# Two weight conversions and a few weight preparations moved to other steps in a Mamba-2 scan with an ELU feed-forward block

## The chip, the cores and the metric

The kernel runs on one core of a Trainium2 chip. The metric is device time in microseconds (us) of one execution, measured without the profiler; the median of several executions stands for a kernel. One further execution was recorded by the profiler, and all times of single instructions come from that one. Instants are counted from the start of its span.

The core's engines work side by side, each through its own list of instructions in a fixed order: PE (matrix products; PEld is its loading of weights), DVE (vector work), ACT (activation functions), POOL (general work), and SP, which here only starts transfers. They wait for each other through semaphores.

## The reference, cut to what matters

The first block is a chunked state-space scan over four batches of eight heads and 768 tokens; its output is laid out as 3072 tokens of 256 numbers. The second block is a feed-forward layer.

```python
h = x @ w_in                                  # (3072, 256) @ (256, 2048)
g = np.where(h > 0.0, h, np.exp(np.minimum(h, 0.0)) - 1.0)
return g @ w_out                              # (3072, 2048) @ (2048, 256)
```

The weights arrive as 64-bit floating point numbers. The kernel has to turn each into a 32-bit one by integer and floating point work on the two 32-bit words of the number.

## The kernel before, in words

**Tiling.** The 3072 tokens are cut into twelve blocks of 256, numbered n = 0 to 11 in order of work. The scan makes the transposed input `yT` of two neighbouring blocks at a time. The feed-forward layer of a block has eight pieces of w_in (256 columns each) and eight pieces of w_out (256 rows each).

**Conversion of the weights.** `pieces` lists sixteen pieces: 0 to 7 are w_in and 8 to 15 are w_out, so that piece 14 holds the rows that the seventh group of second-layer products (`l2(n, 6)`) reads, and piece 15 those of the eighth (`l2(n, 7)`). One conversion is `w_take` and `w_give`: ACT takes the absolute value (L196), DVE scales the low words (L209), cuts out the signs (L223), clips (L231) and puts the high word together (L238), and POOL adds the two parts (L248). The last step writes the finished piece, and PE waits for it.

**First layer.** Blocks 0 to 3 use plain 32-bit products (`l1`, L667). From the second half of block 2 on, the kernel splits each operand into two words that PE can multiply in a faster format (`l1_words`, L787): three passes per group, `both` times `both`, high word of w times y1, and low word of w times y0. `words_of_w(i)` makes the high word of a w_in piece on ACT (L736) and the sum of its words on DVE (L737). `low_of_w(i)` makes the low word on POOL in two halves (L843). `words_of_y` and `both_of_y` do the same for the input, mainly on DVE (L759, L762, L772).

**Second layer.** Blocks 0 and 1 use plain products (`l2`, L827). From block 2 on, pairs of blocks are multiplied together by a seven-product scheme (`second`, L902). It needs sums and differences of w_out's quarters: `differences` writes a11 - a21 on POOL (L843), and `sum_weights` or its single steps (L714) then change a21 in place and write two more sums. `differences(i, ..)` therefore has to stand before `sum_weights` of the same i.

**The scan beside it.** `scan_ahead`, `turn_part`, `scaled`, `scores`, `sums`, `states`, `across` and `inside` make the scan of later blocks: exponentials on ACT (`decay`, L521) followed by a masking on POOL for every second call (L526), transposes and masks on DVE (L453, L461), a scaling of B on POOL (`scaled`, L408), and small products on PE (L541, L571, L616, L634).

**Order of work.** The tile framework is in manual mode: the order on each engine is the order in which the Python lines are executed, and nothing is reordered. The part that changes is the loop over j = 0 to 7 (first layer of blocks 2 and 3, four pieces each, and all of `l2(0, ..)`), the loop over j = 8 to 15 (first layer in words of blocks 2 and 3 together, called step i = j - 8, with `l2(1, ..)`), and the lines between that loop and the first round of `for n in range(4, NP, 2)`.

Before the change, in the loop over j, the conversion of the next piece is taken ahead of `l1` and given behind it at j = 0, 2, 3, 4, 5, so pieces 11 to 15. `words_of_y(2)` and `words_of_w(4)` follow at j = 4, `low_of_w(4)` and `both_of_y(2)` at j = 5, four differences at j = 6, `words_of_w(5)` at j = 7, and `low_of_w(5)` at step i = 0. Two differences each are at i = 2 and i = 5.

Of the kernel before, what the change touches and what calls it, by code (L numbers as in the profile page):

```python
# [32 lines left out]
def kernel(  # L33
# [27 lines left out]
    nc = tc.nc  # L61
# [21 lines left out]
    def psum(shape, name):  # L83
        return p_a.tile(shape, F32, tag="a", name=name)
# [76 lines left out]
    pieces = []  # L161
# [41 lines left out]
    def w_low(i, eng, cols=slice(None)):  # L203
        if eng is nc.scalar:
            eng.activation(
                pieces[i][0][:, :, cols], w_words(i)[0][:, :, cols], ACT.Identity,
                scale=2.0 ** -51, bias=two)
        else:
            eng.tensor_scalar(  # L209
                out=pieces[i][0], in0=w_words(i)[0], scalar1=2.0 ** -51, scalar2=2.0,  # L210
                op0=ALU.mult, op1=ALU.add)
# [387 lines left out]
    def shift(n, v):  # L599


        return 2 * D * v if n else 0

    def across(*ns):


        y = [[psum([P, len(ns), 2, Q], "ps_y") for _ in range(2)] for _ in range(2)]
        for u in (1, 0):
            for at, n in enumerate(ns):
                for v in range(2):  # L610
                    Sx = starts.pop((n, u, v), None)
                    if Sx is None:
                        continue
                    for q in range(4):
                        rows, col = slice(32 * q, 32 * q + 32), (64 * q + shift(n, v)) % P
                        nc.tensor.matmul(  # L616
                            out=y[q // 2][v][col:col + 64, at, u],
                            lhsT=Sx[rows].rearrange("p k d -> p (k d)"),
                            rhs=st[n]["cts"][rows, u, Q * v:Q * v + Q],
                            start=(u == 1 and at == 0), stop=False,  # L620
                            tile_position=(32 * q, col), skip_group_check=True)
        return y

    def inside(y, *ns, t=None):

        for t in range(2) if t is None else (t,):
            for at, n in enumerate(ns):
                s = st[n]
                for u in range(2):
                    for v in range(2):  # L630
                        toks = slice(Q * v, Q * v + Q)
                        for q in range(4):
                            h, col = 4 * t + q, (D * q + shift(n, v)) % P
                            nc.tensor.matmul(  # L634
                                out=y[t][v][col:col + D, at, u],
                                lhsT=s["x"][toks, u, D * h:D * (h + 1)],
                                rhs=s["M"][h // 2][toks, u, h % 2], start=False, stop=True,
                                tile_position=(Q * v, col), skip_group_check=True)
            n = ns[0]
            if n // 2 not in yT:  # L640
                yT[n // 2] = ffn.tile([P, KC, 2, 2, P], F32, tag="yT", name="yT")
            out = yT[n // 2][:, t, n % 2:n % 2 + len(ns)]
            for v in range(2):
                k = shift(n, v)
                for at in (0, k) if k else (0,):
                    count, src = P - k, (at + k) % P
                    to, src = out[at:at + count, :, :, Q * v:Q * v + Q], y[t][v][src:src + count]
                    if t and n == 1:
                        nc.vector.tensor_copy(to, src)
                    else:  # L650
                        nc.scalar.copy(out=to, in_=src)
        if t:
            for n in ns:
                st.pop(n)
# [76 lines left out]
    def words_of_w(i):  # L731

        w = pieces[i][0]
        k_words[i] = conv.tile(
            [P, 2, KC, CW], F32R, tag="w64", name="w_words", bufs=W_AHEAD)
        nc.scalar.activation(k_words[i][:, 0], w, ACT.Copy, scale=NEAR)  # L736
        nc.vector.scalar_tensor_tensor(  # L737
            out=k_words[i][:, 1], in0=k_words[i][:, 0].bitcast(F32), scalar=1.0 / WORD - 1.0,
            in1=w, op0=ALU.mult, op1=ALU.add)

    def low_of_w(i):

        w0 = conv.tile([P, KC, CW], F32R, tag="w_in", name="w0", bufs=DF // CW + 1)
        for k in range(KC):
            sub(w0[:, k], pieces[i][0][:, k], k_words[i][:, 0, k].bitcast(F32))
        k_words[i] = k_words[i], w0
# [20 lines left out]
    def both_of_y(n):  # L767
        y = yT[n // 2].rearrange("p k b u i -> p k (b u i)")
        y1, y0 = y_words[n]
        both = ffn.tile([P, KC, 2 * BLK], F32R, tag="yT", name="y_both")  # L770
        for k in range(KC):
            nc.vector.scalar_tensor_tensor(  # L772
                out=both[:, k], in0=y1[:, k].bitcast(F32), scalar=1.0 - WORD,
                in1=y[:, k], op0=ALU.mult, op1=ALU.add)
        y_words[n] = y1, y0, both
# [66 lines left out]
    def sub(out, in0, in1):  # L842
        nc.gpsimd.tensor_tensor(out=out, in0=in0, in1=in1, op=ALU.subtract)  # L843
# [120 lines left out]
    def w_take(i, low):  # L964

        w_abs(i)
        w_low(i, low)
        w_sign(i)

    def w_give(i):  # L970

        w_high(i)
        w_sum(i)
# [115 lines left out]
    todo = 5  # L1089
# [77 lines left out]
    def differences(i, count):  # L1167
        for r in range(i, i + count):
            sub(s_out[1][:, r], a_out[0][:, r], a_out[2][:, r])

    for j in range(2 * DIRECT):
        n, i = 2 + j // DIRECT, j % DIRECT
        if j < 7:
            l2(0, j)
        piece = todo < len(pieces) and j != 1
        if j == 0:
            elu()
        if piece:
            w_take(todo, nc.vector)
        l1(n, i)  # L1180
        if j == 7:
            l2(0, j)
        if j == 0:
            scaled(3, nc.gpsimd)
            turn(3)
            elu()
            turn_exp(3)
        if piece:
            w_give(todo)
            todo += 1  # L1190
        while lag:
            elu()
        if j == 0:
            decay(3, 2)
            decay(3, 3)
        if j == 1:
            scores(3)
            sums(3)
            for q in range(4):
                weigh(3, q)  # L1200
        if j == 2:
            states(3)
        if j == 3:
            inside(across(3), 3)
        if j == 4:
            words_of_y(2)
        if j == 4:
            words_of_w(4)
        if j == 5:
            low_of_w(4)  # L1210
        if j == 5:
            both_of_y(2)
        scan_ahead(j)
        if j == 3:
            s_out[:] = weight_sums()
        if j == 6:
            differences(0, 4)
        if j == 7:
            words_of_w(5)
    for j in range(8, 16):  # L1220
        i = j - 8
        l1_words(2, j)
        if i == 7:
            words_of_y(4)
        for p in ((), (6,), (), (7,), (0,), (1,), (2,), ())[i]:
            words_of_w(p)
        for p in ((5,), (), (6,), (7,), (0,), (), (), ())[i]:
            low_of_w(p)
        if i == 7:
            l2(1, 6)  # L1230
            l2(1, 7)
        begin_end()
        if i == 0:
            turn_part(5, 2)
            scaled(4, nc.gpsimd)
            scaled(5, nc.gpsimd)
        if i < 2:
            load_bc(i + 6)
            l2(1, i)
        if i == 2:  # L1240
            turn_part(4, 3)
            turn_part(5, 3)
            scores(4, 5)
            sums(4, 5)
            for q in range(4):
                weigh_two(4, q)
            l2(1, 2)
            states(4)
            states(5)
            for to in (6, 7):  # L1250
                load_b(to)
                spread_cum(to)
        if i == 3:
            l2(1, 3)
        if i == 4:
            l2(1, 4)
            y = across(4, 5)
            inside(y, 4, 5)
        if i == 5:
            l2(1, 5)  # L1260
        if i in (0, 1, 3, 4):
            sum_t1(2, (0, 1, 3, 4).index(i), nc.vector)
        if i in (4, 6):
            turn_part(6, i // 2 - 2)
        if i in (2, 5):
            differences(4 if i == 2 else 6, 2)
        if i < 6:
            sum_weights(nc.gpsimd, a_out, s_out, i)
    both_of_y(4)
    end_words()  # L1270
    words_of_w(3)
    decay(6, 0)
    for p in (3, 1, 2):
        low_of_w(p)
    sum_t2(2, 0)
    sub(g_of[2, 14][:, 1], g_of[2, 14][:, 1], g_of[2, 14][:, 0])
    left = (step for i in (6, 7) for step in weight_steps(nc.vector, a_out, s_out, i))
# [105 lines left out]
```

## Time and profile before

| quantity | value |
|---|---|
| device time, median of 3 runs | 351.92 us (351.70 to 352.15) |
| device time of the profiled execution | 351.6 us |
| its span, first to last instruction | 349.5 us |
| PE busy | 340.5 us (97%) |
| DVE, ACT, POOL busy | 259.7, 234.7, 217.2 us |
| granted clock of PE | 1.000 |

The profiled execution lies 0.3 us below the median, and 2.1 us of it lie outside the span. In the views that follow, a row gives the start, the duration, the engine, the line of the kernel, the operation, what is written from what, the shapes and the number of instructions that are merged in it. A bracket at the end of a row gives idle time ahead of it and the instruction that ended it. A row of waits gives the total, the number of waits and the longest one. Ends of matrix products are modelled, so the text uses the starts of the products: of 128x256 in plain format they start 0.216 us apart, of 128x512 in the faster format 0.232 us apart, when nothing holds them up.

### The profile page before, as it was taken

The numbers are of one execution on the slowest core, as the hardware profiler recorded it, in microseconds if no ns is written. First come the engines' busy times: TensorE is split into PE (matmuls) and PEld (weight loads), VectorE is DVE, ScalarE is ACT, GpSimd is POOL, SyncE is SP. The second block draws the span as 40 slices with busy tenths as digits, with TensorE's granted clock in tenths as the row PEclk, the third lists the DMA queues.
The fourth block names the chain that finished last, engine by engine and source line by source line (L and its number), as shares of the span: only waits on it lengthen the run. The fifth ranks groups of instructions, "written<-read, shape, count | busy, mean of one in ns | idle before, by whom it ended". The sixth has DMA issues, their size and how long they took to land.

```text
span 349.5 us, 9873 instructions
## 1 busy us (share of the span) xinstructions
PE 340.5 (97%) x3878; PEld 298.1 (85%) x3878; DVE 259.7 (74%) x515; ACT 234.7 (67%) x537; POOL 217.2 (62%) x338
## 2 busy tenths in 40 slices
PE   8899999998999999999999999999999999999996
PEld 5579888887778899988989988989988999999996
DVE  3998979879997899876878775888675856665232
ACT  4789989697658888657599457599457466565000
POOL 5554554557999599975196764196854174455760
DMA  8988989381360510070431170330000100001002
GB/s 143 247 213 188 296 171 233 81 148 36 70 138 3 110 46 29 10 158 4 105 62 32 13 155 4 89 50 2 2 0 5 62 0 3 0 0 50 15 0 62
DMA packets 72727, 26.49 MB, mean 76 GB/s; under 512 B 57768, under 2 KB 67560, under 8 KB 72680
## 3 DMA queue, kind: packets, MB, share of 16 engines
q1 hardware_dynamic: 70360, 25.60, 31.8%
q8 instruction: 30, 0.49, 0.6%
q10 hardware_dynamic: 2320, 0.26, 0.5%
q14 instruction: 17, 0.14, 0.1%
HBM read 22.51 MB, written 3.34 MB: 74 GB/s over the span
## 4 chain that ended last, share of the span: by engine, by line
PE 83%; DVE 4%; POOL 3%; ACT 3%; SPq 2%; issue 2%; DMA 2%; POOLq 0%; DVEq 0%; ACTq 0%
PE ps_o L902 36%; PE ps_h L787 18%; PE ps_w L787 9%; PE ps_h L667 9%; PE ps_o L827 4%; PE ps_y L634 2%; PE ps_g L541 2%; DMA w<-in_moe_w_in_dram 2%; PE ps_y L616 1%; PE ps_st L571 1%; POOL L L526 1%; POOL w L843 1%; SPq L178 1%; DVE y L762 1%; POOL w_sum L843 1%
## 5 line engine op out<-in xcount | busy, mean ns | idle before, releaser
L902 PEld LDWEIGHTS ps_o<-w_out,g 128*128 128x128 f32 x640 | 78.5, 191 | 3.4
L902 PE MATMUL ps_o<-w_out,g 128*128 128x128 f32 x640 | 80.1, 275 | 0.0
L800 ACT ACTIVATE e<-ps_h 128x512 f32<-128x512 f32 x72 | 43.0, 598 | 47.0 <-DVE ps_h L794 47.0
L808 DVE SCALAR_TENSOR_TENSOR g<-e,ps_h 128x512 f32<-128x512 f32 x72 | 49.4, 686 | 31.9 <-ACT e L801 31.6
L843 POOL TENSOR_TENSOR g<-g 128x256 f32<-128x256 f32 x36 | 26.5, 737 | 58.3 <-DVE g L808 58.2
L794 DVE SCALAR_TENSOR_TENSOR ps_h<-ps_h,e 128x512 f32<-128x512 f32 x72 | 50.1, 695 | 12.4 <-ACT e L791 9.1
L791 ACT ACTIVATE e<-ps_w 128x512 f32<-128x512 f32 x72 | 42.3, 587 | 19.8 <-PE ps_w L787 19.6
L787 PE MATMUL ps_w<-y_both,w_words 128*128 128x512 f32 x144 | 51.5, 437 | 0.1
L801 ACT ACTIVATE e<-e 128x512 f32<-128x512 f32 x72 | 45.5, 632 | 2.3
L667 PE MATMUL ps_h<-yT,w_in 128*128 128x256 f32 (+1 forms) x208 | 45.1, 367 | 1.6 <-POOL w_in L248 1.6
L787 PE MATMUL ps_h<-y,w_words 128*128 128x512 f32 x144 | 45.7, 399 | 0.0
L787 PE MATMUL ps_h<-y,w 128*128 128x512 f32 x144 | 45.0, 392 | 0.2 <-POOL w L843 0.2
L667 PEld LDWEIGHTS ps_h<-yT,w_in 128*128 128x128 f32 x208 | 36.4, 190 | 7.2 <-POOL w_in L248 2.3
L521 ACT ACTIVATE L<-L,ncum 128x64 f32<-128x64 f32 x160 | 42.2, 336 | 0.2
L902 PE MATMUL ps_o<-w_sum,g 128*128 128x128 f32 x304 | 38.6, 276 | 0.0
L902 PEld LDWEIGHTS ps_o<-w_sum,g 128*128 128x128 f32 x304 | 37.0, 192 | 1.4
L526 POOL TENSOR_SCALAR_AFFINE_SELECT L<-L 64x512 f32<-64x512 f32 x40 | 29.3, 732 | 9.6 <-ACT L L521 8.2
L787 PEld LDWEIGHTS ps_h<-y,w 128*128 128x128 f32 x144 | 27.0, 188 | 7.2 <-POOL w L843 0.7
L787 PEld LDWEIGHTS ps_h<-y,w_words 128*128 128x128 f32 x144 | 26.7, 188 | 6.2 <-issue 0.5
L843 POOL TENSOR_TENSOR g<-t,g 128x256 f32<-128x256 f32 x40 | 28.2, 738 | 5.8 <-PE ps_o L902 5.7
L827 PE MATMUL ps_o<-w_out,g 128*128 128x256 f32 x128 | 30.5, 382 | 1.0 <-POOL w_out L248 1.0
L843 POOL TENSOR_TENSOR g<-g,t 128x256 f32<-128x256 f32 x40 | 28.8, 751 | 0.2
(133 smaller groups left out, 538.9 us busy)
## 6 DMA issues: line engine op xcount, KB each, us to landing
L<-flat SPq DMA_DIRECT2D x20, 256.0 KB
w<-in_moe_w_out_dram SPq DMA_DIRECT2D x8, 512.0 KB
w<-in_moe_w_in_dram SPq DMA_DIRECT2D x7, 512.0 KB
xr<-in_x_dram SPq DMA_DIRECT2D x24, 128.0 KB
out_dram<-c_sum SPq DMA_DIRECT2D x9, 256.0 KB
bc<-in_B_dram SPq DMA_DIRECT2D x24, 64.0 KB
bc<-in_C_dram SPq DMA_DIRECT2D x22, 64.0 KB
ec<-flat_exp SPq DMA_DIRECT2D x10, 128.0 KB
```

What stands on the lines that cost most here:

```text
L521: nc.scalar.activation(L[:, h, u], L[:, h, u], ACT.Exp, bias=ncum[:, u, row:row + 1])
L526: nc.gpsimd.affine_select(out=part, in_=part, pattern=[[0, 4], [0, 2], [1, Q]], compare_op=ALU.is_ge, fill=0.0, base=0, channel_multiplier=-1)
L667: nc.tensor.matmul(out=ps[:, j, toks], lhsT=w_in[i][:, k, j * P:(j + 1) * P], rhs=yT[n // 2][:, k, n % 2].rearrange("p u i -> p (u i)")[:, ...
L787: nc.tensor.matmul(out=ps, lhsT=lhs[:, k], rhs=rhs[:, k], start=k == 0 and lhs is not w0, stop=k == KC - 1 and lhs is not w1)
L791: nc.scalar.activation(e, both, ACT.Copy, scale=WORD)
L794: nc.vector.scalar_tensor_tensor(out=high, in0=high, scalar=WORD - 1.0, in1=e, op0=ALU.mult, op1=ALU.add)
L800: nc.scalar.activation(e, high, ACT.Relu, scale=-1.0)
L801: nc.scalar.activation(e, e, ACT.Exp, scale=-1.0)
L808: nc.vector.scalar_tensor_tensor(out=g_of[n, m].rearrange("p b i -> p (b i)"), in0=e, scalar=1.0, in1=h, op0=ALU.subtract, op1=ALU.max)
L827: nc.tensor.matmul(out=o_of[n][:, ts], lhsT=g_of[n, j][:, m % 2, ts * P:(ts + 1) * P], rhs=w_out[:, m], start=(m == 0 and ts == 0), stop=( ...
L843: nc.gpsimd.tensor_tensor(out=out, in0=in0, in1=in1, op=ALU.subtract)
L902: nc.tensor.matmul(out=ps[:, ts], lhsT=b[:, ts * P:(ts + 1) * P], rhs=a[:, i], start=(i == chunk[0] and ts == 0), stop=(i == chunk[-1]), s ...
```

## The change

Piece 14 is converted as a whole at the end of j = 3, behind `inside(across(3), 3)`, and piece 15 at j = 4 behind `words_of_y(2)`; both were taken at the head of the following j. `words_of_w(4)` moves from j = 4 to j = 5 and stands ahead of `both_of_y(2)`. `words_of_w(5)` and `low_of_w(5)` move to j = 6, from j = 7 and from step i = 0. The differences 0 to 3 move from j = 6 to step i = 0, the differences 4 and 5 stay at i = 2, and 6 and 7 move from i = 5 to behind `low_of_w(3)`, ahead of `low_of_w(1)`. No function changes.

```diff
-        piece = todo < len(pieces) and j != 1
+        piece = j in (0, 2, 3)
...
         if j == 3:
             inside(across(3), 3)
+            w_take(14, nc.vector)
+            w_give(14)
         if j == 4:
             words_of_y(2)
-        if j == 4:
+            w_take(15, nc.vector)
+            w_give(15)
+        if j == 5:
             words_of_w(4)
-        if j == 5:
+            both_of_y(2)
             low_of_w(4)
-        if j == 5:
-            both_of_y(2)
         scan_ahead(j)
...
         if j == 6:
-            differences(0, 4)
-        if j == 7:
             words_of_w(5)
+            low_of_w(5)
...
-        for p in ((5,), (), (6,), (7,), (0,), (), (), ())[i]:
+        for p in ((), (), (6,), (7,), (0,), (), (), ())[i]:
             low_of_w(p)
...
-        if i in (2, 5):
-            differences(4 if i == 2 else 6, 2)
+        if i in (0, 2):
+            differences(4 * (i // 2), 4 - i)
...
-    for p in (3, 1, 2):
-        low_of_w(p)
+    low_of_w(3)
+    differences(6, 2)
+    low_of_w(1)
+    low_of_w(2)
```

## The prediction

> **What bounds the kernel now.** The first view is the busy time of the engines: PE works for 97% of the span, so what can be won is PE's idle time. The second is the list of PE's waits over the whole span, which says whom it waits for; PEld rows are the same stalls seen from the weight load.
>
> ```profile
> PE 340.5 (97%) x3878; PEld 298.1 (85%) x3878; DVE 259.7 (74%) x515; ACT 234.7 (67%) x537; POOL 217.2 (62%) x338
> ```
>
> ```profile
> PE ps_y L634 <- issue: 1.7, 4, 0.6
> PE ps_h L667 <- POOL w_in L248: 1.6, 3, 0.8
> ...
> PE ps_o L827 <- POOL w_out L248: 1.0, 1, 1.0
> PE ps_h L787 <- POOL w L843: 0.2, 1, 0.2
> ```
>
> The w_in row belongs to the start, which the change leaves alone. The one w_out wait is piece 15, and "POOL w L843" is a low word. The third view, the timeline around that wait, shows what delays piece 15: DVE does the words of y and w (75.38, 77.06) and a transpose before its four conversion instructions, and POOL's sum comes at 80.55.
>
> ```profile
> 77.06 1.14 DVE L737 SCALAR_TENSOR_TENSOR w_words<-w_words,w_in 128x512 fp32r<-128x512 f32 x1
> ...
> 78.61 0.41 DVE L209 TENSOR_SCALAR w_out<-w 128x512 f32<-128x512 uint32 x1
> ...
> 79.71 0.69 DVE L238 SCALAR_TENSOR_TENSOR mag<-mag,sgn 128x512 uint32<-128x512 uint32 x1
> ...
> 80.55 1.27 POOL L248 TENSOR_TENSOR w_out<-mag,w_out 128x512 uint32<-128x512 uint32 x1 [2.89 <-DVE mag L238]
> 80.92 2.58 DVE L772 SCALAR_TENSOR_TENSOR y_both<-y,yT 128x512 fp32r<-128x512 f32 x2
> 81.78 2.31 POOL L843 TENSOR_TENSOR w<-w_in,w_words 128x256 fp32r<-128x256 f32 x2
> 81.87 1.59 PEld L827 LDWEIGHTS ps_o<-w_out,g 128*128 128x128 f32 x8 [1.41 <-POOL w_out L248]
> ```
>
> PE's last first-layer product starts at 80.49, so the next could start at 80.70; it starts at 81.87. That stall is **1.17**. Later a product of group (2,10) starts at 91.50 instead of 91.09, waiting for the low word of piece five (POOL's row at 89.97): **0.41**.
>
> The fourth view is POOL's timeline behind the loop: idle until 117.63, then without a pause to 146.
>
> ```profile
> 113.47 0.46 POOL L714 TENSOR_TENSOR w_sum<-w_out,w_sum 128x128 f32<-128x128 f32 x1
> 117.63 5.35 POOL L843 TENSOR_TENSOR w<-w_in,w_words 128x256 fp32r<-128x256 f32 x6 [3.70 <-ACT w_words L736]
> 122.94 2.83 POOL L843 TENSOR_TENSOR t<-g 128x256 f32<-128x256 f32 x4
> ...
> 143.61 1.39 POOL L526 TENSOR_SCALAR_AFFINE_SELECT L<-L 64x512 f32<-64x512 f32 x2
> 145.09 0.64 POOL L408 TENSOR_TENSOR b_tok<-b_tok,eb 128x256 f32<-128x256 f32 x1
> ```
>
> **The change part by part.** No instruction is added or removed, and no DMA is issued at another step: SP's order is untouched, and ACT and POOL start no transfers here. Nothing is priced by its own duration, only by what waits for it.
>
> *Piece 14.* ACT's absolute value (0.67) passes eight exponentials (0.24 apart) and starts at 69.85 instead of 71.78; the next activation, at 72.35, has the same work ahead of it. DVE's clip then runs at 70.6 and its last step ends at 71.7; POOL's sum (1.27) ends at 73.1 instead of 75.06. PE reads the piece at 75.52, so both are hidden. POOL's two maskings (70.99) move behind the sum to 74.5, DVE's transpose (69.18) to 72.3; they are next needed at 95 and 84. Cost 0.
>
> *Piece 15.* ACT's absolute value moves from 75.50 to 74.0, ahead of the word of w. DVE: the words of y start at 74.2 as before. They took 1.11, 0.69 and 1.14; a free one of 128x512 with two operands takes 0.69 (the row of 115.3), so they end between 76.1 and 77.1, the first if POOL is idle, which it is now after 74.5. The four conversion steps take 1.8 (78.61 to 80.40), POOL follows 0.15 later with 1.27: ready between 79.3 and 80.3, needed at 80.70. The cover is 0.4 even at the slow end. **Gain 1.17.**
>
> *Words of w four, both of y, low word of four.* They now follow the conversion, so PE needs them earlier: l2(0,7) would end at 82.43, where the first group in words starts. DVE after 77.9: transpose 0.65, an ELU step 0.68, words of w, two halves of both-of-y. The two halves bound each other with POOL:
>
> ```profile
> L772 DVE SCALAR_TENSOR_TENSOR y_both<-y,yT x2: 687/687/687, 115.3 to 115.9; 128x512 fp32r<-128x512 f32 x2
> ```
> ```profile
> L772 DVE SCALAR_TENSOR_TENSOR y_both<-y,yT x2: 1209/1329/1449, 80.9 to 82.3; 128x512 fp32r<-128x512 f32 x2
> ```
>
> The first row is with POOL idle, the second beside the two low-word instructions: each half ends 0.55 after a POOL instruction ended (81.82, 82.95), and the next POOL instruction ends 0.58 after the half. They take turns. In the new order they meet POOL's sum (to 79.3) and two maskings of 0.67; taking turns gives words of w at 79.84 and the halves at 80.92 and 82.00. Free, they would end at 81.0; with the 1.45 and 1.21 of before, at 82.7. Need 82.43: cost 0 to 0.3, taken 0. The low word follows on POOL, its halves at 82.6 and 83.3, needed at 83.36 and 83.59 (third pass): cost 0 to 0.2, taken 0.
>
> The Trainium skill, "SBUF — State Buffer", section "Who interferes with whom", calls this an exclusive lock of a port that DVE and GpSimd share, held for a whole instruction by whoever starts first, and so says that more POOL work beside DVE costs whole instructions. The rows agree that turns are taken. Read at its worst, with a neighbour of 1.27 instead of 0.67 for both halves, the estimate is 83.2 and a loss of 0.8; by the rows it is 0.
>
> *Words and low word of five.* Their ACT part fills an idle stretch (ACT sat idle for 2.51 ahead of 83.90). DVE's word stands ahead of the last ELU step at 84.3 instead of 87.16; that step waits for its exponential until 84.4 and then 0.5 for the word. POOL's low word (0.79 and 0.73) follows two maskings and ends by 86.9 instead of 91.45; PE needs it at 90.86 - 1.17 = 89.7. **Gain 0.41.** Behind it in POOL's queue wait two maskings and the two scalings of B (0.8 each), done at 89.9 instead of 93.27; the small products that read them stall some 0.1 at 93.24. Gain 0.1.
>
> DVE decides whether this holds: from 87.16 to 100 it has no idle time, and PE's group (2,11) starts at 95.90 and 96.56 right after DVE's second and fourth weighting product (95.76, 96.42). Without the word of five (0.72) and with ACT earlier, DVE's first step there goes from 87.80 to 86.1: 1.7 as well. Between 1.3 and 1.9 by collisions, taken 1.7.
>
> *Differences 0 to 3* leave POOL at 86.03 (2.16) and come after the scalings, at 89.9 to 91.7. The weight sums and the low word of six behind them end at 97.2, needed at 100.22 - 1.7 = 98.5. Cost 0.
>
> *Differences 6 and 7* leave 111.10, where POOL later idles 3.70, and enter the unbroken stretch. Four of them at 86.03 start 0.42 apart; the contended one at 111.52 took 0.92. So POOL is later by 0.83, between 0.8 and 1.85. Next late: the second half of the low word of one, ready at 121.48, goes to 122.27; PE can see it at 122.32 and wants it at 122.19: cost 0.13. Then the scaling of the B of block 7 (row 145.09, ready at 145.73): PE loads it at 145.91, 0.07 after the load before, so the slack is some 0.1. At a lateness of 0.7 (some turns with DVE fall better) PE waits **0.6**; bounds 0, if turns absorb all, and 1.75. DVE's steps 6 and 7 (L714, 125.11) need the differences by then and have them.
>
> Sum: 1.17 + 0.41 + 0.1 - 0.13 - 0.6 = 0.95, so the profiled execution goes from 351.6 to 350.65. The median lies 0.32 above it: **350.95**.
>
> **The rivals.**
> A: the late POOL work is absorbed. For it: about 2 us of that stretch are turns with DVE (118.32 took 1.19 for 0.73), which fall anew. Against: no pause in 28 us. Gain 1.68: 350.25.
> B: DVE comes late at 82 and in the steps that follow, 0.5 in all, by unlucky turns. For it: the small cover of 0.4. Then the gain is 0.45: 351.45, no difference to see.
> C, slower: POOL's stretch from 117.63. Two contended differences (1.85) and two more collisions like the one at 133.74 (1.22 for 0.73, so 0.49 each) make the scaling 2.8 late; PE waits 2.7 at 145.9 and ends 1.1 behind: 353.0. It turns the sign from a lateness of 1.65, and shows as slower from 2.4. Against: only two of the 37 instructions up to the scaling are extra.
> D: the stalls only move, for example into the 0.85 at 104.99, where the profile names "issue" and no engine; gain 0.2: 351.7.
>
> **How the numbers follow.** The forecast has 0.45, A 0.22, B 0.20, C 0.08, D 0.05. Faster by over 0.2% (0.70 us, about what a measurement of this kernel can tell) means below 351.22: A and three quarters and more of the forecast's own range of 350.5 to 351.4, 0.60. Same takes B, D and the rest, 0.31; slower 0.09. The range of 350.0 to 351.8 takes in A, B and D and leaves C out.
>
> **What would show it.** Right: PE's w_out wait is gone; the sum of piece 15 ends before 80.0; the both-of-y rows end by 82.4; PE's wait for "w L843" at 91 is gone; a new PE wait for POOL appears at the sums near 144. Wrong: PE waits for DVE y_both near 82.5, or DVE's weighting products move up by less than 1.3, or the new wait at the sums is absent (A) or above 1.6 (C).

## The result, and the profile after

The changed kernel takes **350.53 us** (median of 7 runs, 349.88 to 351.0) beside 351.92 for the kernel before on the same chip. The ratio is 0.9954 with a 95% interval of 0.9939 to 0.9969: faster by 0.3 to 0.6%. Put beside three other kernels later, it gave 350.41 against 351.74, ratio 0.9966 (0.9952 to 0.998). The forecast was 350.95.

The line of busy times, and the whole list of PE's waits in the changed kernel (us in total, times, longest):

```profile
PE 341.0 (98%) x3878; PEld 298.4 (86%) x3878; DVE 257.9 (74%) x515; ACT 234.7 (67%) x537; POOL 216.5 (62%) x338
```
```profile
PE ps_y L634 <- issue: 1.6, 4, 0.6
PE ps_h L667 <- POOL w_in L248: 1.6, 3, 0.8
PE ps_idle L263 <- DVE idle L258: 1.1, 1, 1.1
```

The wait for w_out (1.0 before) is gone from the list, and so is the one for "w L843" at 91. What stands there still is the start and the "issue" stalls (PE idle while the profile names no engine that it waits for), which the change does not touch. The timeline around the old stall shows why, first in the kernel before, then in the changed one (rows of other work in between are left out):

```profile
73.79 1.27 POOL L248 TENSOR_TENSOR w_out<-mag,w_out 128x512 uint32<-128x512 uint32 x1 [1.40 <-DVE mag L238]
...
74.24 1.11 DVE L759 TENSOR_SCALAR y<-yT 128x512 fp32r<-128x512 f32 x1
...
75.38 1.75 DVE L762 SCALAR_TENSOR_TENSOR y<-y,yT 128x512 fp32r<-128x512 f32 x2
```

```profile
74.57 0.47 DVE L759 TENSOR_SCALAR y<-yT 128x512 fp32r<-128x512 f32 x1
...
75.08 1.29 DVE L762 SCALAR_TENSOR_TENSOR y<-y,yT 128x512 fp32r<-128x512 f32 x2
...
76.29 0.42 DVE L209 TENSOR_SCALAR w_out<-w 128x512 f32<-128x512 uint32 x1
...
78.25 1.28 POOL L248 TENSOR_TENSOR w_out<-mag,w_out 128x512 uint32<-128x512 uint32 x1 [3.49 <-DVE mag L238]
...
79.48 2.19 POOL L526 TENSOR_SCALAR_AFFINE_SELECT L<-L 64x512 f32<-64x512 f32 x2
80.00 2.20 DVE L772 SCALAR_TENSOR_TENSOR y_both<-y,yT 128x512 fp32r<-128x512 f32 x2
...
81.09 1.89 PE L827 MATMUL ps_o<-w_out,g 128*128 128x256 f32 x8
81.75 2.26 POOL L843 TENSOR_TENSOR w<-w_in,w_words 128x256 fp32r<-128x256 f32 x2
...
84.06 0.19 PEld L787 LDWEIGHTS ps_h<-y,w 128*128 128x128 f32 x1 [0.36 <-POOL w L843]
```

Piece 15's sum ends at 79.53; PE reads the piece at 81.09, straight behind its product. The words of y run from 74.57 to 76.37, in 1.80, where they took 2.89 before (74.24 to 77.13), since POOL is idle beside them from 74.76 on. Both of y ends at 82.20, and PE's first group in words starts at 82.63 without a wait for it. The low word of four ends at 84.01, and the third pass of that group waits for its second half at 84.06: a new, small stall.

Three later places carry costs. The first is on DVE (its timeline near 98): the sixth state of blocks 4 and 5 waits 0.71 for POOL's masked states, which stand behind the differences and the low word of six. The first line is POOL's, from its own timeline.

```profile
90.91 1.88 POOL L843 TENSOR_TENSOR w_sum<-w_out 128x128 f32<-128x128 f32 x4
```
```profile
98.36 0.28 DVE L588 SCALAR_TENSOR_TENSOR S_new<-S_new,ec,ps_st 128x64 f32<-128x64 f32 x1 [0.71 <-POOL Sx L593]
98.55 0.68 DVE L808 SCALAR_TENSOR_TENSOR g<-e,ps_h 128x512 f32<-128x512 f32 x1
```

Before, the six states ran through without a wait, and the ELU step behind them began at 99.37:

```profile
97.67 1.79 DVE L588 SCALAR_TENSOR_TENSOR S_new<-S_new,ec,ps_st 128x64 f32<-128x64 f32 x6
...
99.37 0.68 DVE L808 SCALAR_TENSOR_TENSOR g<-e,ps_h 128x512 f32<-128x512 f32 x1
```

So DVE is ahead by 0.82 here, where it was ahead by 1.42 at the first state. The second place follows from it: PE's first group in words of blocks 4 and 5, near 115, waits longer for both of y. The third is POOL's stretch from 116.09, with differences 6 and 7 in it:

```profile
116.09 1.87 POOL L843 TENSOR_TENSOR w<-w_in,w_words 128x256 fp32r<-128x256 f32 x2 [3.41 <-ACT w_words L736]
117.93 1.32 POOL L843 TENSOR_TENSOR w_sum<-w_out 128x128 f32<-128x128 f32 x2
119.21 2.93 POOL L843 TENSOR_TENSOR w<-w_in,w_words 128x256 fp32r<-128x256 f32 x4
...
144.03 0.64 POOL L408 TENSOR_TENSOR b_tok<-b_tok,eb 128x256 f32<-128x256 f32 x1
```

The scaling of block 7's B starts 1.06 sooner than before (145.09), PE's sums there come 1.29 sooner. Within the sums PE's products now stand 0.27 apart ahead of the one at 144.50, where they stood 0.12 apart before. That product still belongs to block 6, and the load for it (144.47) comes 0.12 behind a step of DVE, the last of `c_sum` (to 144.35); in the kernel before, it came 0.12 behind the same step too (to 145.49). In a second profile of the changed kernel (changed_again below) this step is in time, and PE pauses at the change from block 6 to block 7 instead: the two loads stand 0.56 apart, and the second, at 145.16, comes 0.06 behind the end of the scaling.

```profile
143.60 0.75 DVE L880 TENSOR_TENSOR c_sum<-ps_o,c_sum 128x256 f32<-128x256 f32 x2
```
```profile
PE ps_st L571 <- POOL b_tok L408: 0.3, 1, 0.3
```

The first row is from the first profile, the second from the waits of the second. In the first, too, the scaling (to 144.67) would have held block 7's load until some 144.73; it came at 144.77. So two waits of nearly the same size lie on top of each other here.

**How the runs below are compared.** Single parts are worth 0.1 to 0.7 us, and the interval of a ratio is 0.4 to 0.7 us to either side. So the parts are read from PE, whose order is the same in all kernels here: the time between the starts of the same two matmuls, less that time in the kernel before. The stretches, by the clock of the kernel before: a, 80.49 to 82.41, piece 15; b, to 85.30, the first group in words; c, to 92.09, up to the low word of five; d, to 94.33, the sums of blocks 4 and 5; e, to 114.01, without 104.02 to 105.07, which holds an "issue" stall; f, to 117.20, the first group in words of blocks 4 and 5; g, to 143.07; h, to 146.62, the sums of blocks 6 and 7. All in us against the kernel before, with the ratio of the times:

| kernel | a | b | c | d | e | f | g | h | sum | ratio (95%) |
|---|---|---|---|---|---|---|---|---|---|---|
| changed | -1.27 | +.20 | -.52 | -.28 | +.04 | +.24 | +.01 | +.15 | -1.44 | .9954 (.9939, .9969) |
| changed_again | -1.27 | +.27 | -.53 | -.26 | +.08 | +.28 | .00 | +.17 | -1.27 | .9966 (.9952, .9980) |
| conv_alone | -1.27 | +.29 | +.68 | -.29 | -.36 | +.21 | .00 | -.20 | -.94 | .9978 (.9966, .9990) |
| words_alone | -.01 | .00 | -.55 | -.29 | -.03 | +.03 | +.11 | +.24 | -.49 | .9987 (.9972, 1.0002) |
| piece14_back | -1.27 | +.84 | -.51 | -.29 | -.36 | +1.04 | +.01 | -.15 | -.69 | .9969 (.9952, .9987) |
| diff_spread | -1.27 | +.26 | -.53 | -.27 | -.14 | +.25 | .00 | +.19 | -1.50 | .9956 (.9940, .9971) |
| state_bufs | -1.27 | +.27 | -.53 | -.26 | +.09 | +.08 | +.06 | +.27 | -1.29 | .9944 (.9925, .9963) |
| diff67_back | -1.27 | +.26 | -.55 | -.24 | +.10 | +.26 | +.01 | -.20 | -1.64 | .9976 (.9964, .9989) |
| diff67_twice | -1.27 | +.30 | -.53 | -.26 | +.05 | +.30 | +.68 | +.36 | -.37 | .9985 (.9971, 1.0000) |
| low4_early | -1.27 | -.01 | -.55 | +.10 | +.09 | +.27 | +.02 | +.20 | -1.15 | .9959 (.9945, .9973) |
| conv15_first | -1.27 | +.78 | -.55 | -.24 | -.23 | .00 | +.15 | +.32 | -1.05 | .9970 (.9958, .9983) |
| bufs_and_dve | -1.27 | +.27 | -.53 | -.27 | +.06 | .00 | +.71 | +.66 | -.38 | 1.0018 (1.0006, 1.0031) |
| all_three | -1.27 | +.75 | -.52 | -.26 | -.18 | -.01 | +.74 | +.67 | -.09 | 1.0020 (1.0008, 1.0033) |

The first two rows are two profiles of one kernel. They agree within 0.07 in every stretch, and within 0.17 in the sum; a difference below that between two rows is not read. The start, up to 80.49, varies more: it is 0.10 shorter to 0.93 longer than that of the kernel before, in code that no row changes, and the "issue" stall near 104 is 0.38 shorter to 0.14 longer. A profile's own span therefore says less than this sum.

### The profile page after: what moved, and what is told of

Same layout as the page of the kernel before. It is cut to its first block, busy times and chain, and to the rows that moved or that the text cites. A ratio compares the mean times of both kernels' runs of the same rounds, so it can differ in the third digit from the quotient of the medians.

```text
span 348.6 us, 9875 instructions
## 1 busy us (share of the span) xinstructions
PE 341.0 (98%) x3878; PEld 298.4 (86%) x3878; DVE 257.9 (74%) x515; ACT 234.7 (67%) x537; POOL 216.5 (62%) x338
## 4 chain that ended last, share of the span: by engine, by line
PE 87%; ACT 3%; DVE 3%; SPq 2%; DMA 2%; issue 1%; POOL 0%; POOLq 0%; ACTq 0%
PE ps_o L902 36%; PE ps_h L787 18%; PE ps_h L667 11%; PE ps_w L787 9%; PE ps_o L827 6%; PE ps_y L634 2%; DMA w<-in_moe_w_in_dram 2%; PE ps_g L541 2%; PE ps_y L616 1%; PE ps_st L571 1%; DVE ps_h L794 1%; ACT e L800 1%; SPq L178 1%; ACT yT L651 1%; ACT e L801 1%
## 5 line engine op out<-in xcount | busy, mean ns | idle before, releaser
L808 DVE SCALAR_TENSOR_TENSOR g<-e,ps_h 128x512 f32<-128x512 f32 x72 | 49.3, 685 | 31.9 <-ACT e L801 30.4
L843 POOL TENSOR_TENSOR g<-g 128x256 f32<-128x256 f32 x36 | 27.3, 758 | 58.5 <-DVE g L808 58.4
L791 ACT ACTIVATE e<-ps_w 128x512 f32<-128x512 f32 x72 | 42.2, 586 | 20.1 <-PE ps_w L787 20.0
L843 POOL TENSOR_TENSOR g<-t,g 128x256 f32<-128x256 f32 x40 | 28.2, 737 | 5.8 <-PE ps_o L902 5.7
L843 POOL TENSOR_TENSOR g<-g,t 128x256 f32<-128x256 f32 x40 | 28.6, 748 | 0.2
```

Source lines behind the costliest of these rows:

```text
L791: nc.scalar.activation(e, both, ACT.Copy, scale=WORD)
L808: nc.vector.scalar_tensor_tensor(out=g_of[n, m].rearrange("p b i -> p (b i)"), in0=e, scalar=1.0, in1=h, op0=ALU.subtract, op1=ALU.max)
```

## The experiments

The diffs are against the changed kernel.

**The change once more, and its two halves.** The repeat (changed_again) has no edit.

> The changed kernel once more, beside the three others of this group. It tells what of a profile repeats. Expected: from PE's last first-layer product ahead of the second one of piece 15 to the end of the sums of blocks 6 and 7, leaving out the stall within the small products near 104, 1.4 to 1.5 less than the kernel before, as in the first profile; the start and the stalls within the small products differ by up to 0.5. Time 350.5.

Time as expected; the sum came out at 1.27, a little under the 1.4 to 1.5 expected, and the stall left out 0.16 shorter than before.

The conversions alone:

```
         if j == 6:
-            words_of_w(5)
-            low_of_w(5)
+            differences(0, 4)
+        if j == 7:
+            words_of_w(5)
...
-        for p in ((), (), (6,), (7,), (0,), (), (), ())[i]:
+        for p in ((5,), (), (6,), (7,), (0,), (), (), ())[i]:
             low_of_w(p)
...
-        if i in (0, 2):
-            differences(4 * (i // 2), 4 - i)
+        if i in (2, 5):
+            differences(4 if i == 2 else 6, 2)
...
-    differences(6, 2)
```

> Pieces 14 and 15, the words of four and both of y as in the changed kernel; the words and the low word of five and all differences as before. Theory (the conversions bring the 1.17, the words of five the rest): PE's wait for w_out is gone, its wait for the low word of five stays and grows, because PE arrives 1 us sooner and DVE, which still holds the word of five among the last ELU steps, moves by about 1.0 only. Time 350.9 to 351.4, 0.5 to 1.0 below the kernel before and some 0.6 above the changed one. Rival 1 (the conversions bring everything): 350.5, as the changed kernel. Rival 2 (the stall only moves to the low word of five): 351.7 to 351.9.

The words of five and the differences alone:

```
-        piece = j in (0, 2, 3)
+        piece = todo < len(pieces) and j != 1
...
-            w_take(14, nc.vector)
-            w_give(14)
...
-            w_take(15, nc.vector)
-            w_give(15)
-        if j == 5:
             words_of_w(4)
-            both_of_y(2)
+        if j == 5:
             low_of_w(4)
+        if j == 5:
+            both_of_y(2)
```

> The words and low word of five and the differences as in the changed kernel; pieces 14 and 15, the words of four and both of y as before. Theory: PE's wait for w_out stays at 1.0 to 1.2, the 0.41 at the low word of five is gone, the moved differences cost up to 0.4 behind it: 351.5 to 352.0, no difference to the kernel before that can be told. Rival (POOL's and DVE's relief at the words of five brings most of the gain): 351.0 or less.

Measured: 351.04 us for the conversions, 351.27 for the words, beside 351.72. PE's waits from 78 to 95, first with the conversions alone, then with the words alone:

```profile
PE ps_h L787 <- POOL w L843: 0.6, 1, 0.6
```
```profile
PE ps_o L827 <- POOL w_out L248: 1.0, 1, 1.0
```

Each half leaves the other's stall. With the conversions alone the wait for the low word of five grows, as expected of PE coming sooner, but 0.36 of that comes back in e, at the products that started right behind DVE's weighting products before (95.90 and 96.56). The sums are 0.94 and 0.49; together 1.43, beside 1.27 and 1.44 for the whole change. So the two halves add up, two thirds and one third, and both rivals that give all to one half fall. The time of the words alone is 0.2 below the range expected, and the interval of its ratio takes in no change, so for that half the waits and the sum speak, not the time.

**What piece 14's place is worth.**

```
-        piece = j in (0, 2, 3)
+        piece = j in (0, 2, 3, 4)
...
             inside(across(3), 3)
-            w_take(14, nc.vector)
-            w_give(14)
```

> The changed kernel with piece 14 converted around the first-layer product of step 4, as before, and piece 15 at its new place. Theory (only piece 15 was late; piece 14 has over a microsecond in hand wherever it stands): PE has no wait for w_out of over 0.1, time 350.5. Rival (piece 14 had to leave, because its steps stand ahead of the words of y and of piece 15 on DVE and POOL): piece 15's sum ends past PE's need, a wait for w_out of 0.2 to 0.8 comes back, 350.7 to 351.3.

351.14 us beside 352.0. PE has no wait for w_out, as the theory has it, but the first group in words waits 0.84 (b), and the group at f 1.04, where the changed kernel lost 0.2 and 0.24. Neither side expected that. The timeline (DVE and POOL) shows where it starts:

```profile
74.50 1.28 POOL L248 TENSOR_TENSOR w_out<-mag,w_out 128x512 uint32<-128x512 uint32 x1 [1.38 <-DVE mag L238]
74.95 1.11 DVE L759 TENSOR_SCALAR y<-yT 128x512 fp32r<-128x512 f32 x1
76.10 1.29 DVE L762 SCALAR_TENSOR_TENSOR y<-y,yT 128x512 fp32r<-128x512 f32 x2
...
79.22 1.28 POOL L248 TENSOR_TENSOR w_out<-mag,w_out 128x512 uint32<-128x512 uint32 x1 [3.43 <-DVE mag L238]
```

Piece 14's sum now stands on POOL beside DVE's first word of y, as in the kernel before. It has 0.83 left when that word starts, and the word takes 1.11 instead of 0.47 (there POOL's masking had 0.19 left). In the kernel before, in the changed one and here the word ends 0.28 or 0.29 behind POOL's instruction. That 0.64 reaches piece 15 and everything behind it on POOL: its maskings, the low word of four, and the masked states. DVE's wait from 92 to 100:

```profile
DVE S_new L588 <- POOL Sx L593: 1.7, 1, 1.7
```

So moving piece 14 matters, by some 0.6 to 0.75 of the sum, though PE never waited for that piece.

**The differences 0 to 3, and the state that waits.** The first run computes each difference just ahead of the sum that uses it:

```
-        if i in (0, 2):
-            differences(4 * (i // 2), 4 - i)
         if i < 6:
+            differences(i, 1)
             sum_weights(nc.gpsimd, a_out, s_out, i)
```

> The changed kernel, but each of differences 0 to 5 is computed just ahead of the weight sum that needs it, so that one and not four of them stand ahead of the low word of six and the masked states on POOL. Theory: DVE's wait of 0.7 for POOL's Sx at 98.4 is gone or under 0.2, DVE's both-of-y for blocks 4 and 5 ends 0.3 to 0.7 sooner, PE's pause at its first group in words of blocks 4 and 5 falls from 0.24 beyond that of the kernel before to about 0: 350.3, 0.2 below the changed kernel. Rival 1: the state waits for the low word of six itself and not for the differences ahead of it: the 0.7 stays above 0.4, 350.5. Rival 2: the 0.24 is won and is lost again at the sums of blocks 6 and 7 (pause there 0.4): 350.5.

350.3 us beside 351.72. The state's wait falls to 0.3, but f stays at +0.25. Here another thing takes its place, seen on DVE (first fence) and POOL (second):

```profile
112.93 1.55 DVE L762 SCALAR_TENSOR_TENSOR y<-y,yT 128x512 fp32r<-128x512 f32 x2 [0.22 <-ACT y L757]
114.41 1.28 DVE L772 SCALAR_TENSOR_TENSOR y_both<-y,yT 128x512 fp32r<-128x512 f32 x2
```
```profile
113.07 0.87 POOL L714 TENSOR_TENSOR w_sum<-w_out,w_sum 128x128 f32<-128x128 f32 x1
```

POOL's last weight sum meets the low word of y, whose two halves take 1.55 instead of 1.29 (a half 0.94 instead of 0.69). The same is seen with the conversions alone (1.51) and with differences 6 and 7 at step 5 (1.58), and f is +0.21 to +0.26 in all three (in the last the state still waits 0.7). So f was no proof of the state's wait, and the next run asks for it by itself:

```
-            new = att.tile([P, 2, D], F32, tag="S", name="S_new", bufs=6)
+            new = att.tile([P, 2, D], F32, tag="S", name="S_new", bufs=7)
...
-            Sx = att.tile([P, 2, D], F32, tag="Sx", name="Sx", bufs=12)
+            Sx = att.tile([P, 2, D], F32, tag="Sx", name="Sx", bufs=11)
```

> The changed kernel with seven buffers instead of six for the states and eleven instead of twelve for the masked states. It tells what DVE's sixth state of blocks 4 and 5 waits for, and what that wait is worth. Theory A (the sixth state waits for the buffer that POOL's masked states free): the wait of 0.7 is gone, DVE's ELU step behind it starts 0.6 sooner against PE, and the pause of PE at its first group in words of blocks 4 and 5 (0.26 above that of the kernel before) goes to under 0.1. Theory B (POOL's last weight sum sets a floor there, as in the runs with a separate conversion and with spread differences, where one half of the low word of y took 0.91 to 0.94 instead of 0.69): the wait of 0.7 is gone, one half of the low word of y takes over 0.85, and the pause stays at 0.2 to 0.3. Theory C: the wait is no matter of buffers, and stays at 0.6 to 0.7. Time 350.3 by A, 350.5 by B and C.

350.17 us beside 352.0, and DVE's timeline there:

```profile
96.18 1.72 DVE L588 SCALAR_TENSOR_TENSOR S_new<-S_new,ec,ps_st 128x64 f32<-128x64 f32 x6
97.82 0.68 DVE L808 SCALAR_TENSOR_TENSOR g<-e,ps_h 128x512 f32<-128x512 f32 x1
...
112.46 1.39 DVE L762 SCALAR_TENSOR_TENSOR y<-y,yT 128x512 fp32r<-128x512 f32 x2 [0.22 <-ACT y L757]
```

The six states run through without the wait, so it was one for a buffer. f falls to +0.08, and in the two later runs with these buffers to 0.00, while one half of the low word of y loses 0.1 to POOL. That is A, for the most part. But h rises from +0.15 to +0.27, and the sum stays where it was: what PE gains at f it waits for at the sums. The profile gives that wait to DVE's `c_sum`, but the scaling (to 144.62) would have held block 7's load until some 144.68, and it came at 144.70; against the product at f, the scaling comes no sooner than in the changed kernel.

```profile
PE ps_st L571 <- DVE c_sum L880: 0.2, 1, 0.2
```

**The differences 6 and 7.** Back at step 5, and twice in their new place:

```
-        if i in (0, 2):
-            differences(4 * (i // 2), 4 - i)
+        if i in (0, 2, 5):
+            differences(*{0: (0, 4), 2: (4, 2), 5: (6, 2)}[i])
...
-    differences(6, 2)
```

> The changed kernel, but differences 6 and 7 are computed at step 5 again, where POOL idles later. Theory (the trace: the scaling of the B of block 7 is 0.16 late for the sums): the 0.25 pause of PE at the sums of blocks 6 and 7 goes, 350.35, 0.1 to 0.2 below the changed kernel. Rival 1, the forecast's own price (0.6 and 0.13): 349.8. Rival 2, the lateness is only the turns with DVE and comes back elsewhere: 350.5, no change, and the pause stays.

```
     differences(6, 2)
+    differences(6, 2)
```

> The changed kernel with differences 6 and 7 computed twice in their new place, which adds two POOL instructions of 0.45 to 0.92 to the unbroken stretch. Theory (a lateness there counts one for one at the sums of blocks 6 and 7): PE's pause there grows from 0.25 to 1.0 to 1.3, time 351.3. Rival (turns with DVE absorb it): the pause stays under 0.5, time 350.6.

Back at step 5: 350.96 us beside 351.72. The pause at the sums is gone, h is -0.20, 0.35 to 0.37 better than in the two profiles of the changed kernel: both the scaling and `c_sum` are in time. (The 0.16 in the expectation sets the scaling against the product at 144.50, which is block 6's.) The time, 0.6 above the theory's, does not show it, as 0.35 us is less than the interval of the ratio; that the ratio came out above the changed kernel's has no counterpart in these stretches.

Twice: 351.57 us beside 352.0. The waits from 117 to 147:

```profile
PE ps_st L571 <- POOL b_tok L408: 0.5, 1, 0.5
...
PE ps_h L787 <- POOL w L843: 0.2, 1, 0.2
```

Two more instructions (2.16 for the four, 1.32 for the two) cost 0.9 to 1.07 of the sum: one for one, as the theory says, and a little more. But most of it falls at the low word of one (g, +0.68), and only then at the sums (h, +0.36), where the products stand 0.70 apart and not the 1.0 to 1.3 of the theory.

**Attempts to win more.** The low word of four sooner:

```
             w_give(15)
+            words_of_w(4)
+            low_of_w(4)
         if j == 5:
-            words_of_w(4)
             both_of_y(2)
-            low_of_w(4)
```

> The changed kernel with the words and the low word of piece four issued right behind piece 15, ahead of the maskings of that step. Theory: PE's pause of 0.2 at the third pass of its first group in words (wait for the low word of four) is gone, and that is kept to the sums of blocks 4 and 5: 350.3. Rival: the low word now meets the words of w and the halves of both of y on DVE, so the first pass waits for both of y instead, 0.1 to 0.6: 350.5 to 351.0.

350.52 us beside 352.0. The stall at b is gone (-0.01), and both of y is not late. The price comes elsewhere: the sums of blocks 4 and 5 wait again (d is +0.10 instead of -0.28). POOL's maskings and the scalings of B are later, but the scalings still end at 91.38, 0.76 ahead of the first load of the sums (92.14). What comes late is the ELU step on DVE:

```profile
89.70 1.68 POOL L408 TENSOR_TENSOR b_tok<-b_tok,eb 128x256 f32<-128x256 f32 x2
```
```profile
91.62 0.69 DVE L808 SCALAR_TENSOR_TENSOR g<-e,ps_h 128x512 f32<-128x512 f32 x1
```

Counted from PE's first load of the scores just ahead of the sums, this step ends at 1.55 here, at 1.16 in the changed kernel and at 1.44 in the kernel before. The differences, 0.38 and 0.28, are those of d. What made the step late is not followed further.

Piece 15 ahead of the words of y:

```
-            words_of_y(2)
             w_take(15, nc.vector)
             w_give(15)
+            words_of_y(2)
```

> The changed kernel with piece 15 converted ahead of the words of y instead of behind them. POOL's sum then ends near 78 and its maskings and the low word of four can start sooner, while the words of y come 1.8 later on DVE. Theory A (the pause at the low word of four is POOL's chain behind piece 15): the pause of 0.2 goes, both of y ends within 0.3 of where it ends now, 350.3. Theory B (the words of y now stand beside POOL's sum and maskings and take 0.4 to 0.6 longer each): both of y ends after 82.6, and PE waits for it 0.3 to 0.8 ahead of its first group in words: 350.8 to 351.3.

350.78 us beside 351.74: B. The low word of y stands beside POOL's sum and masking and takes 2.70 for two halves instead of 1.29, and PE waits for both of y:

```profile
77.18 2.70 DVE L762 SCALAR_TENSOR_TENSOR y<-y,yT 128x512 fp32r<-128x512 f32 x2
```
```profile
PE ps_w L787 <- DVE y_both L772: 0.5, 1, 0.5
```

The buffers as above, and differences 6 and 7 on DVE:

```
-    differences(6, 2)
...
-    left = (step for i in (6, 7) for step in weight_steps(nc.vector, a_out, s_out, i))
+    def last_sums(i):
+        yield lambda: nc.vector.tensor_tensor(
+            out=s_out[1][:, i], in0=a_out[0][:, i], in1=a_out[2][:, i], op=ALU.subtract)
+        yield from weight_steps(nc.vector, a_out, s_out, i)
+
+    left = (step for i in (6, 7) for step in last_sums(i))
...
-                for _ in range(2):
+                for _ in range((2, 3, 3)[k - 2]):
                     next(left)()
```

> The changed kernel with seven and eleven buffers for the states and masked states, and with differences 6 and 7 computed by DVE in the stage behind, just ahead of their weight sums, instead of by POOL. Theory (the two costs that the change brought are the state's wait for a buffer and the lateness at the sums of blocks 6 and 7): PE's pause at the first group in words of blocks 4 and 5 is within 0.1 of that of the kernel before, the pause at the sums is gone, and the same stretch is 1.8 to 2.0 below that of the kernel before: 350.1. Rival (DVE is full there: two more instructions on it make its steps late): PE or ACT waits for DVE between 124 and 136, and the stretch is 1.3 to 1.5 below: 350.5 to 350.7.

352.49 us beside 351.74: slower than the kernel before. f is 0.00, but g and h lose 1.37, where they lose 0.33 with the buffers alone. DVE's two differences, and PE's waits from 117 to 147:

```profile
L1280 DVE TENSOR_TENSOR w_sum<-w_out x2: 783/804/825, 124.3 to 128.7; 128x128 f32<-128x128 f32 x2
```
```profile
PE ps_st L571 <- DVE c_sum L880: 0.6, 1, 0.6
PE ps_o L902 <- ACT c_sum L939: 0.4, 1, 0.4
```

A DVE instruction of this shape takes 0.28 where POOL's instruction beside it has only 0.12 left (127.75 in the same timeline); these took 0.78 and 0.82, with 0.63 and 0.68 left. Against PE's product at f, DVE's steps behind them come later by 0.8 and then by 1.5 than with the buffers alone. The rival's mechanism holds, at a price well above the one it was given.

All together (the edits of the last two):

> Piece 15 ahead of the words of y, the additional buffers, and differences 6 and 7 on DVE, together. Where A of the run before and the theory of the run with buffers and DVE both hold, the stretch is 2.0 to 2.2 below that of the kernel before and the time 349.9; where B holds, it is that of the buffers and DVE less what both of y loses, 350.4 to 350.9.

352.75 us beside 351.74: both losses, at b (+0.75) and at g and h (+1.41), and so a time above both expectations. No kernel was found that beats the changed one: the fastest median, 350.17 with the additional buffer, has an interval that overlaps the changed kernel's.

## Why the prediction was right, point by point

The likeliest case, its sign and its mechanism held: DVE and POOL were late with piece 15 and with the low word of five, and both stalls went. The working gave 0.95, the two profiles 1.27 and 1.44 over the stretch it speaks of, and the time fell by 1.39 and 1.33. (By its own sum the forecast is 351.92 - 0.95 = 350.97; it says 350.95.) That the total came so close is in part luck. Terms that were priced came out better than priced by 0.96 in the first profile (a 0.10, c 0.11, d 0.18, g 0.12, h 0.45), and places that were priced at nothing lost 0.48 (b 0.20, e 0.04, f 0.24). The terms, with instants of the first profile of the changed kernel, whose start is 0.39 longer than that of the kernel before:

- *Piece 15, 1.17.* Measured 1.17 at the load and 1.27 over stretch a. The sum ended at 79.53, which is 79.14 on the clock of the kernel before, just ahead of the 79.3 to 80.3 worked out; DVE's words took the short end, with POOL idle beside nearly all of them.
- *Piece 14, 0.* The step that failed, though not in the total: it asked only whether PE would see piece 14 late. Its real effect is on the neighbour: with its sum at the old place the first word of y takes 1.11 and not 0.47, and 0.58 to 0.75 of the gain is lost (shown by piece14_back). The prediction had named the idle POOL as the condition for the fast end, but not as the worth of this edit.
- *Both of y, 0 to 0.3, taken 0.* Right: it ended at 82.20, worked out as needed at 82.43.
- *Low word of four, 0 to 0.2, taken 0.* Mis-sized: b lost 0.20 and 0.27. Its halves ended at 82.79 and 84.01, or 82.40 and 83.62 on the clock of the kernel before, where 82.6 and 83.3 were worked out. Each ended 0.6 behind the DVE instruction beside it, the first behind both of y (to 82.20), the second behind a masking of the scan (L461, to 83.40), which the working left out.
- *Low word of five, 0.41, and 0.1 at the sums.* c gained 0.52, and the wait is gone. At the sums the gain was 0.28, but not for the reason given. In the kernel before, the first load of the sums (93.21) comes 0.07 behind an ELU step on ACT (L791, to 93.14), and the load behind a pause of 0.14 (93.42) comes 0.05 behind the ELU step on DVE (L808, to 93.37). Both distances are the same in low4_early, where the scalings are done in good time. So the ELU steps held PE there; the scalings did not.
- *DVE must hold 1.7.* It did: its weighting products came 1.42 sooner in a profile whose start was 0.39 longer, so 1.81, inside 1.3 to 1.9.
- *Differences 0 to 3, cost 0.* Wrong in its ground. The weight sums and the low word of six behind them were in time, as said; but behind the low word stand the masked states, and DVE's sixth state needs a buffer that they free. The wait was 0.7, and 0.16 to 0.20 of it reached PE at f (state_bufs). The working looked at who reads the moved work and the work behind it, not at who waits for a buffer.
- *Differences 6 and 7: 0.13 at the low word of one, 0.6 at the sums.* Mis-sized. g lost nothing, h 0.15 to 0.17; compared with the same kernel without this move (diff67_back), the pause costs 0.35 to 0.37. The sign that was to show it, a new wait of PE for POOL at the sums, stands in the second profile; in the first, DVE's `c_sum` hides it, a wait that the working did not have. From the start of POOL's stretch to the scaling it took 27.94 beside 27.46 before: the two differences took 1.32 but added only 0.48, and not 0.83, because the six low halves took 4.80 instead of 5.35 and the rest 0.29 less. Rival A's mechanism, turns that fall anew, thus held in part. The loss at f made PE later too, and so hid part of the price: with 0.16 of f mended, h rises by 0.12.

Rival B (DVE late) did not come; it is what conv15_first made. Rival C's price for lateness on POOL is right, one for one and more (diff67_twice), but its two collisions did not happen. D came in small: b, f and h took back 0.59 and 0.72, though not at the "issue" stall that it named.

The Trainium skill, "SBUF — State Buffer", section "Who interferes with whom", has DVE and GpSimd exclude each other from a shared port for whole instructions. The rows here agree: the first word of y took 0.47 where POOL's instruction had 0.19 left and 1.11 where it had 0.83 left, and a sum of 128x128 took 0.28 with 0.12 left and 0.78 with 0.63 left. The rule told that there would be turns, but their order decided the sums, and that came from the trace.

Open: why the start and the "issue" stalls inside the small products (0.49 to 1.01 between two products near 104) differ between executions, and why `c_sum` comes late in one profile of the changed kernel and not in the other.

## What to carry to other kernels

When work is moved between engines that take turns at memory, ask not only who reads it late but which instruction it stood beside: piece 14 had slack in plenty, and its old place cost some 0.6 through a neighbour. Behind every instruction that is delayed, look also for buffers that it frees, not only for results. And price a place on a full engine before filling it: two differences that took 1.3 us on POOL took 1.6 on DVE, and cost PE about 1.0 more.

## What the runs showed that was not expected

- The first word of y (one operand, 128x512) took 0.47 with POOL all but idle and 1.11 beside a POOL sum of 1.28, and the low word of y 2.70 instead of 1.29 for two halves. The word of y ended 0.28 or 0.29 behind POOL's instruction in each of three profiles: here the delay was what was left of that instruction, not a share of speed.
- Stalls that were mended one at a time came back elsewhere: 0.16 won at f by a buffer returned as 0.12 at h; 0.21 to 0.28 won at b by an earlier low word returned as 0.36 to 0.38 at d.
- Two different causes, a state that waits for a buffer and a low word of y that meets POOL's last weight sum, gave 0.21 to 0.28 at the same place of PE. At the sums of blocks 6 and 7, DVE's `c_sum` in one profile and POOL's scaling in the other gave 0.15 and 0.17. The size of a stall did not tell its cause.
